# A two-layer GELU network on one core: the engines' instructions emitted without a block

## The chip, the core and the metric

The kernel runs on one core of one Trainium2 chip. The metric is the device time of one execution in microseconds (us). A core has five engines with an instruction stream each: TensorE (PE), VectorE (DVE), ScalarE (ACT), GpSimd (POOL) and SyncE (SP). They meet only through semaphores; transfers between memory and the core's own buffers are DMAs that SP, ACT or POOL issue and that add to a semaphore when they land.

## What is computed

```python
def reference(x, w1, b1, w2, b2):          # x: 1 x 2048 x 448
    h = jnp.einsum("bsd,df->bsf", x, w1) + b1   # w1: 448 x 1792
    h = _gelu(h)                                # tanh approximation
    return jnp.einsum("bsf,fd->bsd", h, w2) + b2   # w2: 1792 x 448
```

All inputs and the output are bfloat16. There are 2048 tokens of 448 numbers, a hidden layer of 1792, and an output as large as the input.

## The kernel before

The first product makes the hidden layer transposed: 14 tiles of 128 hidden features by four chunks of 512 tokens, 56 tiles `g_sb` in all. TensorE accumulates each in one of eight PSUM banks (L265), ScalarE applies bias and GELU on the way to `g_sb` (L366). The depth of 448 is cut into three slices of 128 rows and one of 64, and the 64-row slices of two tiles are paired, so that each pair of tiles costs seven passes. The second product takes 128 tokens at a time: 14 matmuls over the hidden features (L339), then VectorE adds the second bias on the way to `out_sb` (L389), and a store goes out (`store`, L166 to L169). There are 16 token tiles; the last is cut into 320 and 128 columns, so that there are 17 stores. TensorE does the whole first product (`l1`), then the whole second (`l2` for the four chunks), in an order written out by hand.

The beginning is staged so that TensorE has work early. It runs twelve warm-up matmuls on constants (L238), then turns the first 512 tokens by matmuls with an identity matrix (L248), while the weights arrive; VectorE and ScalarE copy the turned tokens out of PSUM (L378, L362). POOL makes the identity (L224, L226) and issues one small DMA (L231). The other tokens come in through transposing DMAs.

SP issues nearly all transfers in this order: the first tokens (L207, L208), pieces of the first weights (L180, L185, L186, L189), the transposing loads (L199), the second weights (L193), the second bias (L216), and then, as each VectorE addition is done, the stores (L169) but for the last, which ScalarE issues (L371). SP's last act is the wait for all 17 stores (L220), 16 counts of `sem_od` each.

Constants and a first barrier of all engines are made when the program object is created (L406): POOL sets four constants; each engine drains and reports to a gathering semaphore; POOL waits for four reports and releases the four others.

Line 160 opens a block, and each engine's function is registered with it by a decorator (L205, L222, L233, L353, L373). The block is closed where the `with` of L121 ends. In the program as built, the main body then holds only the constants, the first barrier and one unconditional branch per engine; each engine's work is a body of its own that ends with another branch; and a common end body holds a second barrier of the same form as the first (a drain on each engine, POOL's two events, an event on each of the others). The instructions of that end carry line 121. SP's wait for the stores is attached to its branch to the end body.

Of the kernel before, what the change touches and what calls it, by code (L numbers as in the profile page):

```python
# [11 lines left out]
def bass_standalone__dense_activation_gelu__prompt_kernel(  # L12
# [78 lines left out]
    for i in range(OPENING, len(order), QUAD):  # L91
# [3 lines left out]
        steps += phase(i + 2, 0) + phase(i, 1) + phase(i + 2, 1)  # L95
    assert len(set(steps)) == len(steps)
    assert sum((1 + h // 2) * (t1 - t0) for _, h, _, (t0, t1) in steps) == len(order) // 2 * 7 * SC


# [5 lines left out]
    for n, (i, h, m, _) in enumerate(steps):  # L105
        before = ahead.get(i)
        turn.append(before if before is not None and {steps[before][1], h} == {0, 1} else None)
        ahead[i] = n
        starts.append(before is None)
# [11 lines left out]
    with ExitStack() as es:  # L121
# [35 lines left out]
        sem_osb = S_("sem_osb")  # L157
        sem_od = S_("sem_od")

        block = es.enter_context(nc.Block())  # L160


        x0_view = x2[0:SC, :].rearrange("(p t) d -> p t d", t=STC)
        out0_view = out2[0:SC, :].rearrange("(p t) d -> p t d", t=STC)
# [1 line left out]
        def store(eng, n):  # L166
            j, c0, c1 = outs[n]
            to = out0_view[:, j, c0:c1] if j < STC else out2[j * P:(j + 1) * P, c0:c1]
            eng.dma_start(to, out_sb[:, j, c0:c1]).then_inc(sem_od, 16)  # L169

        def x_part(n, parts):
            h, k = parts[0]
            to = xT_sb[:, k:k + len(parts), 2 * h * P:2 * (h + 1) * P]
            src = ps[XBANK[n]][:, 0:2 * P * len(parts)]
            return to, src.rearrange("p (k t) -> p k t", k=len(parts))

        def load_w10(eng, i):
            a, b = W0_PIECES[i]
            with nc.allow_non_contiguous_dma(reason="w1 column pieces"):
                eng.dma_start(w1_sb[:, 0, a * P:b * P], w1[0:P, a * P:b * P]).then_inc(sem_w10[i], 16)  # L180

        def load_w1(eng):
            with nc.allow_non_contiguous_dma(reason="w1 column pieces"):
                for k, r in list(enumerate(KROW))[1:]:
                    eng.dma_start(w1_sb[:, k, 0:WCUT], w1[r:r + P, 0:WCUT]).then_inc(sem_w1[k], 16)  # L185
                eng.dma_start(  # L186
                    w1_sb[:, 0:3, WCUT:F], w1[0:3 * P, WCUT:F].rearrange("(k p) f -> p k f", p=P)
                ).then_inc(sem_w1r, 16)
                eng.dma_start(w1_sb[:, 3, WCUT:F], w1[KROW[3]:D, WCUT:F]).then_inc(sem_w1r, 16)  # L189

        def load_w2(eng, i):
            a, b = W2_PIECES[i]
            eng.dma_start(  # L193
                w2_sb[:, a:b, :], w2[a * P:b * P, :].rearrange("(ft p) d -> p ft d", p=P)
            ).then_inc(sem_w2[i], 16)

        def load_xT(eng, c):
            for k, d0 in enumerate(KROW):
                eng.dma_start(  # L199
                    xT_sb[:, k, c * SC:(c + 1) * SC],  # L200
                    x2[c * SC:(c + 1) * SC, d0:d0 + P],
                    transpose=True,
                ).then_inc(sem_x[c], 16)

        @block.sync  # L205
        def _(sp):
            sp.dma_start(xn_sb[:, 0:2, :], x0_view[:, 0:2, :]).then_inc(sem_xn[0], 16)  # L207
            sp.dma_start(xn_sb[:, 2:4, :], x0_view[:, 2:4, :]).then_inc(sem_xn[1], 16)  # L208
            load_w10(sp, 1)
            load_w1(sp)  # L210
            load_xT(sp, 1)
            for c in range(2, NSC):
                load_xT(sp, c)
            for i in range(len(W2_PIECES)):
                load_w2(sp, i)
            sp.dma_start(b2_bc[:, :], b2.partition_broadcast(P)).then_inc(sem_b2, 16)  # L216
            for n in range(len(outs) - 1):
                sp.wait_ge(sem_osb, n + 1)
                store(sp, n)
            sp.wait_ge(sem_od, 16 * len(outs))  # L220

        @block.gpsimd  # L222
        def _(pool):
            pool.memset(ident[:, :], 0.0).then_inc(sem_id, 1)  # L224
            pool.wait_ge(sem_id, 1)
            pool.affine_select(  # L226
                out=ident[:, :], in_=ident[:, :], compare_op=ALU.not_equal, fill=1.0,
                base=0, pattern=[[-1, P]], channel_multiplier=1,
            ).then_inc(sem_id, 1)

            pool.dma_start(b1n_sb[NFT:SQ, :], w1[0:SQ - NFT, 0:P]).then_inc(sem_b1x, 16)  # L231

        @block.tensor  # L233
        def _(pe):
            ones_w = nc.const_aps.tensor(1.0, [P, P], BF16)
            ones_x = nc.const_aps.tensor(1.0, [P, WN], BF16)
            for _i in range(NWARM):
# [90 lines left out]
            def l2(c):  # L328
                pe.wait_ge(sem_g, NFT * (c + 1))
                for n, (j, c0, c1) in enumerate(outs):  # L330
                    if j // STC != c:
                        continue
                    free("o", n)
                    for ft in range(NFT):
                        if j == 0:
                            for i, (a, _) in enumerate(W2_PIECES):
                                if ft == a:
                                    pe.wait_ge(sem_w2[i], 16)
                        mm = pe.matmul(  # L339
                            bank("o", n)[:, 0:c1 - c0],  # L340
                            lhsT=g_sb[:, ft, j * P:(j + 1) * P],
                            rhs=w2_sb[:, ft, c0:c1],
                            start=(ft == 0), stop=(ft == NFT - 1),
                        )
                    mm.then_inc(sem_l2, 1)
# [4 lines left out]
            for c in range(NSC):  # L350
                l2(c)

        @block.scalar  # L353
        def _(act):
            act.dma_start(b1n_sb[0:NFT, :], b1.rearrange("(c p) -> c p", p=P)).then_inc(sem_b1n, 16)
            load_w10(act, 0)
            zero = nc.const_aps.tensor(0.0, [P, 8], FP32)
            act.activation(act_junk[:, :], zero, ACT.Gelu_apprx_tanh)  # L358
            for n, (e, parts) in enumerate(XPARTS):
                if e == "a":  # L360
                    act.wait_ge(sem_xtp, n + 1)
                    act.copy(*x_part(n, parts)).then_inc(sem_xTa, 1)  # L362
            act.wait_ge(sem_b1, 1)
            for i, (c, ft) in enumerate(order):
                act.wait_ge(sem_l1, i + 1)
                act.activation(  # L366
                    g_sb[:, ft, c * SC:(c + 1) * SC], bank("g", i)[:, :], ACT.Gelu_apprx_tanh,
                    bias=b1_f[:, ft:ft + 1], scale=1.0,
                ).then_inc(sem_g, 1)
            act.wait_ge(sem_osb, len(outs))  # L370
            store(act, len(outs) - 1)  # L371

        @block.vector  # L373
        def _(dve):
            for n, (e, parts) in enumerate(XPARTS):
                if e == "d":
                    dve.wait_ge(sem_xtp, n + 1)
                    dve.tensor_copy(*x_part(n, parts)).then_inc(sem_xTd, 1)  # L378
            dve.wait_ge(sem_b1n, 16)
            dve.wait_ge(sem_b1x, 16)  # L380
            for q in range(P // SQ):
                to = slice(q * SQ, (q + 1) * SQ)
                dve.transpose(b1t_sb[to, :], b1n_sb[:, to]).then_inc(sem_b1T, 1)  # L383
            dve.wait_ge(sem_b1T, P // SQ)
            dve.tensor_copy(b1_f[:, :], b1t_sb[:, 0:NFT]).then_inc(sem_b1, 1)  # L385
            dve.wait_ge(sem_b2, 16)
            for n, (j, c0, c1) in enumerate(outs):
                dve.wait_ge(sem_l2, n + 1)
                dve.tensor_tensor(  # L389
                    out=out_sb[:, j, c0:c1], in0=bank("o", n)[:, 0:c1 - c0], in1=b2_bc[:, c0:c1],  # L390
                    op=ALU.add,
                ).then_inc(sem_osb, 1)


# [26 lines left out]
```

## Time and profile before

| | us |
|---|---|
| median of three runs | 94.45 (94.42 to 94.81) |
| the profiled execution | 93.88 |
| its span, first to last instruction of the program | 92.1 |
| TensorE busy | 89.1 |
| ScalarE busy | 36.6 |
| VectorE busy | 12.2 |

The span is shorter than the execution's time because the runtime has work of its own around the program. TensorE's granted clock was 1.00 throughout. In the profile's rows, a group is named by source line, engine, operation and tiles (out<-in), then a count; PEld is TensorE's loading of weights, which overlaps its matmuls; a name with a q behind it (SPq, ACTq) is an engine's sequencer, which waits, branches and issues DMAs and is not counted as busy. The chain of waits is followed back from the last instruction: each piece is shown with its start, its length and what ran. In the view of one line's instructions, the three numbers are the shortest, median and longest duration in ns, followed by the first and last start in us. Times are counted from the first instruction of the program. Apart from instructions, the trace holds the time of every update of a semaphore, those of the runtime ahead of the program and behind it too.

### The profile page before, as it was taken

Reading aid. Unit: us, or ns where it says so; the run is one execution under the profiler, and the core shown is the slowest. Engines: PE = TensorE matmul, PEld = TensorE weight load, DVE = VectorE, ACT = ScalarE, POOL = GpSimd, SP = SyncE. Lnnn points to the kernel's source line nnn. Section 1 sums busy time; section 2 is a strip of 40 time slices with the busy share of each in tenths; the row PEclk is TensorE's granted clock in tenths of the full one; section 3 lists DMA queues with packets and bytes.
Section 4 is the critical chain, followed back from the end, with each engine's and each line's share of the span. In section 5 each row is a group of like instructions: output and inputs, shape, how many; then the busy total and the mean of one; then the engine's idle time right before and its main releaser. Section 6 shows DMA issues by size and latency. Waiting matters only on the chain.

```text
span 92.1 us, 1498 instructions
## 1 busy us (share of the span) xinstructions
PE 89.1 (97%) x650; PEld 47.2 (51%) x650; DVE 12.2 (13%) x25; ACT 36.6 (40%) x61; POOL 1.4 (1%) x7
## 2 busy tenths in 40 slices
PE   6999999999999999999999999999999999999990
PEld 4664445555555555555545555555555555555570
DVE  0260000000000000000001112222211222222131
ACT  2640999877887779777973000000000000000000
POOL 5000000000000000000000000000000000000000
PEclk9999999999999999999999999999999999999999
DMA  1999988554893000000000111101111110011111
GB/s 24 343 332 333 154 148 73 114 108 74 271 368 104 0 0 4 7 0 0 0 0 0 50 57 50 42 7 50 50 50 50 50 50 29 28 50 50 50 50 50
DMA packets 12562, 7.52 MB, mean 82 GB/s; under 512 B 7171, under 2 KB 12172, under 8 KB 12556
## 3 DMA queue, kind: packets, MB, share of 16 engines
q1 hardware_dynamic: 12208, 7.26, 31.1%
q10 hardware_dynamic: 316, 0.17, 0.6%
q8 instruction: 5, 0.08, 0.3%
q0 software_dynamic: 32, 0.00, 0.1%
q14 instruction: 1, 0.01, 0.0%
HBM read 4.02 MB, written 1.84 MB: 64 GB/s over the span
## 4 chain that ended last, share of the span: by engine, by line
PE 97%; DVE 0%; issue 0%
PE ps L265 46%; PE ps L339 46%; PE ps L238 3%; PE ps L248 1%; DVE out_sb L389 0%
## 5 line engine op out<-in xcount | busy, mean ns | idle before, releaser
L265 PE MATMUL ps<-xT_sb,wi_sb 64*128 64x512 bf16 (+2 forms) x384 | 42.8, 374 | 0.0
L339 PE MATMUL ps<-wo_sb,g_sb 128*128 128x448 bf16 (+2 forms) x238 | 42.6, 341 | 0.0
L366 ACT ACTIVATE g_sb<-ps,bi_f 128x512 bf16<-128x512 f32 x56 | 33.7, 694 | 9.5 <-PE ps L265 9.5
L339 PEld LDWEIGHTS ps<-wo_sb,g_sb 128*128 128x128 bf16 x238 | 22.7, 98 | 20.1 <-issue 0.4
L265 PEld LDWEIGHTS ps<-xT_sb,wi_sb 64*128 64x128 bf16 (+1 forms) x384 | 21.7, 94 | 20.5 <-issue 0.6
L389 DVE TENSOR_TENSOR out_sb<-ps,bo_bc 128x448 bf16<-128x448 f32 (+2 forms) x17 | 10.1, 597 | 73.8 <-PE ps L339 73.8
L238 PE MATMUL ps<-const-bfloat16-1.0 128*128 128x256 bf16 x12 | 2.7, 413 | 0.8 <-PEq L406 0.8
L238 PEld LDWEIGHTS ps<-const-bfloat16-1.0 128*128 128x128 bf16 x12 | 1.6, 140 | 1.4 <-issue 0.8
L358 ACT ACT_TABLE_LOAD x1 | 1.3, 1283 | 1.8 <-issue 1.8
L362 ACT CAST xT_sb<-ps 128x512 bf16<-128x512 f32 (+1 forms) x3 | 1.4, 516 | 1.2 <-PE ps L248 1.2
L378 DVE CAST xT_sb<-ps 128x256 bf16<-128x256 f32 x3 | 1.2, 421 | 4.1 <-PE ps L248 3.9
L248 PEld LDWEIGHTS ps<-ident,xn_sb 128*128 128x128 bf16 x16 | 1.2, 112 | 0.5 <-issue 0.5
L248 PE MATMUL ps<-ident,xn_sb 128*128 128x128 bf16 x16 | 1.4, 244 | 0.0
L383 DVE STREAM_TRANSPOSE bit_sb<-bin_sb 32x32 bf16<-32x32 bf16 x4 | 0.8, 200 | 0.1
L231 POOL DMA_DIRECT2D bin_sb<-in_w_dram x1 | 0.7, 657 | 0.2 <-issue 0.2
L226 POOL TENSOR_SCALAR_AFFINE_SELECT ident<-ident 128x128 bf16<-128x128 bf16 x1 | 0.3, 287 | 0.2 <-POOL ident L224 0.2
L358 ACT ACTIVATE act_junk<-const-float32-0.0 128x8 bf16<-128x8 f32 x1 | 0.2, 209 | 0.0
L224 POOL MEMSET ident<- 128x128 bf16 x1 | 0.2, 204 | 0.3 <-POOLq L406 0.3
L385 DVE CAST bi_f<-bit_sb 128x14 f32<-128x14 bf16 x1 | 0.2, 176 | 0.0
L406 POOL MEMSET const-float32-0.0<- 128x1 f32 x1 | 0.1, 99 | 0.2 <-issue 0.2
L406 POOL MEMSET const-bfloat16-1.0<- 128x1 bf16 x1 | 0.1, 102 | 0.0
L406 POOL MEMSET const-uint8-127<- 128x1 uint8 x1 | 0.1, 102 | 0.0
(1 smaller groups left out, 0.1 us busy)
## 6 DMA issues: line engine op xcount, KB each, us to landing
out_dram<-out_sb SPq DMA_DIRECT2D x15, 112.0 KB, 1.7
wo_sb<-in_w_dram SPq DMA_DIRECT2D x2, 784.0 KB, 6.0
wi_sb<-in_w_dram SPq DMA_DIRECT2D x3, 256.0 KB, 4.0
wi_sb<-in_w_dram SPq DMA_DIRECT2D x1, 576.0 KB, 6.4
xn_sb<-in_x_dram SPq DMA_DIRECT2D x2, 224.0 KB, 2.7
wi_sb<-in_w_dram SPq DMA_DIRECT2D x1, 192.0 KB, 6.6
xT_sb<-in_x_dram SPq DMA_TRANSPOSE x12, 3.6
wi_sb<-in_w_dram ACTq DMA_DIRECT2D x1, 128.0 KB, 2.9
```

Of the source, the lines that this page charges most:

```text
L231: pool.dma_start(b1n_sb[NFT:SQ, :], w1[0:SQ - NFT, 0:P]).then_inc(sem_b1x, 16)
L238: pe.matmul(ps[0][:, 0:WN], lhsT=ones_w, rhs=ones_x, start=True, stop=True)
L248: mm = pe.matmul(ps[XBANK[n]][:, col:col + P], lhsT=xn_sb[:, 2 * h + t, KROW[k]:KROW[k] + P], rhs=ident[:, :], start=True, stop=True,)
L265: return pe.matmul(bank("g", i)[:, t0:t1], lhsT=w1_sb[lo:hi, k, ft * P:(ft + 1) * P], rhs=xT_sb[lo:hi, k, c * SC + t0:c * SC + t1], start= ...
L339: mm = pe.matmul(bank("o", n)[:, 0:c1 - c0], lhsT=g_sb[:, ft, j * P:(j + 1) * P], rhs=w2_sb[:, ft, c0:c1], start=(ft == 0), stop=(ft == NF ...
L358: act.activation(act_junk[:, :], zero, ACT.Gelu_apprx_tanh)
L362: act.copy(*x_part(n, parts)).then_inc(sem_xTa, 1)
L366: act.activation(g_sb[:, ft, c * SC:(c + 1) * SC], bank("g", i)[:, :], ACT.Gelu_apprx_tanh, bias=b1_f[:, ft:ft + 1], scale=1.0,).then_inc( ...
L378: dve.tensor_copy(*x_part(n, parts)).then_inc(sem_xTd, 1)
L383: dve.transpose(b1t_sb[to, :], b1n_sb[:, to]).then_inc(sem_b1T, 1)
L389: dve.tensor_tensor(out=out_sb[:, j, c0:c1], in0=bank("o", n)[:, 0:c1 - c0], in1=b2_bc[:, c0:c1], op=ALU.add,).then_inc(sem_osb, 1)
L406: nc = _bacc.Bacc("TRN2", target_bir_lowering=False, num_devices=1)
```

## The change

The block is not opened. The five decorated functions become plain functions that are called once each at the end of the kernel, with the engine as argument, so that their instructions stand in the program's main body. Within each engine, the order of the working instructions, their operands and their semaphores stay. In the program as built, the five branches into the engines' bodies, the five branches out of them and the end body's barrier (five drains, six events) are gone; the first barrier stays. SP's wait for the stores, which the branch to the end body carried, is an event instruction of its own, the last in SP's stream.

```diff
-        block = es.enter_context(nc.Block())
-
...
-        @block.sync
-        def _(sp):
+        def sync_work(sp):
...
             sp.wait_ge(sem_od, 16 * len(outs))
 
-        @block.gpsimd
-        def _(pool):
+        def gpsimd_work(pool):
...
-        @block.tensor
-        def _(pe):
+        def tensor_work(pe):
...
-        @block.scalar
-        def _(act):
+        def scalar_work(act):
...
-        @block.vector
-        def _(dve):
+        def vector_work(dve):
...
+        sync_work(nc.sync)
+        gpsimd_work(nc.gpsimd)
+        tensor_work(nc.tensor)
+        scalar_work(nc.scalar)
+        vector_work(nc.vector)
```

## The prediction

> **What bounds the kernel now.** I read the page first, then the chain of waits, then the last microseconds, because the change touches only how each engine enters and leaves its work. The page:
>
> ```profile
> span 92.1 us, 1498 instructions
> ...
> PE 89.1 (97%) x650; PEld 47.2 (51%) x650; DVE 12.2 (13%) x25; ACT 36.6 (40%) x61; POOL 1.4 (1%) x7
> ...
> q8 instruction: 5, 0.08, 0.3%
> q14 instruction: 1, 0.01, 0.0%
> ```
>
> TensorE is busy 97% of the span, so a change that leaves its matmuls alone can work only at the two ends. The chain that ended last, in order of time, ends so:
>
> ```profile
> 5.33 42.02 PE ps L265 x380
> 47.35 42.53 PE ps L339 x238
> 89.88 0.02 issue
> 89.90 0.29 DVE out_sb L389
> ```
>
> The chain has no hole between 0.79 and 90.19. What is left is 0.79 us ahead of it and 92.10 - 90.19 = 1.91 us behind it. The timeline of the end and the instructions of line 121, which is where the block is closed (POOLq, SPq and so on are the sequencers):
>
> ```profile
> 89.90 0.29 DVE L389 TENSOR_TENSOR out_sb<-ps,bo_bc 128x128 bf16<-128x128 f32 x1 [0.29 <-PE ps L339]
> 90.22 0.35 ACTq L169 DMA_DIRECT2D out_dram<-out_sb  x1
> ```
>
> ```profile
> L121 POOLq EVENT_SEMAPHORE  x2: 17/17/17, 91.9 to 92.0; - x2
> ...
> L121 SPq COMPARE_BRANCH  x1: 33/33/33, 91.7 to 91.7; - x1
> L121 SPq DRAIN  x1: 7/7/7, 91.9 to 91.9; - x1
> L121 SPq EVENT_SEMAPHORE  x1: 17/17/17, 92.0 to 92.0; - x1
> L121 ACTq EVENT_SEMAPHORE  x1: 17/17/17, 92.0 to 92.0; - x1
> ...
> L121 PEldq EVENT_SEMAPHORE  x1: 51/51/51, 92.0 to 92.0; - x1
> ```
>
> And what SP waited for:
>
> ```profile
> SPq L121 <- DMA out_dram<-out_sb: 1.7, 1, 1.7
> ...
> SPq L121 <- PEq L121: 0.2, 1, 0.2
> ```
>
> The reader is to see a ladder. The last store is issued at 90.22 and lands at 91.71 (semaphore updates in the trace); SP's branch, which carries the wait for the stores, runs at 91.727; SP's drain at 91.883; POOL, which gathers the five engines, at 91.916 and 91.994; the four others are let go at 92.036 to 92.047; TensorE's event ends the span at 92.098. Everything from 91.727 on is the block's end and does no work.
>
> **The start.** The change removes one branch per engine behind the first barrier. That barrier (line 406) stays. I cost the branch at nothing, because it isn't there: the trace has no branch record on any engine at the start, and PE's first weight load starts 77 ns after the barrier's event (0.679 to 0.756), exactly what lies between event and weight load at 3.421, 4.403, 7.656 and 11.669 inside PE's stream, where there is no branch. The other engines show 85 ns (SP) and 88 ns (ACT) from event to first DMA issue, and 119 ns on POOL from the release to the first memset. The nearest rows without a branch are ACT's 68 ns from an event to an activation and POOL's 79 ns between its two events. So the bounds of the gain are 0 and 0.04 us, and even that is behind cover: PE's twelve warm-up matmuls (line 238) start the chain and run until 3.5 us whatever POOL, SP and ACT do. Below nothing there is no reason in the rows. I take 0.
>
> The Trainium skill, "Runtime: NRT & Kernel Launch", section "Instruction fetch mechanics", says that a taken branch to code outside the current window forces a fetch before the engine can go on, so by it five removed branches could each be worth a fetch. The 77 ns above is against it here.
>
> **The end within the span.** What goes: SP's branch as a carrier of the wait (a plain event takes its place, 17 ns by SP's row), SP's drain, POOL's two events, the events of the other four, and drains and branches of engines that are done earlier anyway (DVE's drain starts at 89.916, ACT's at 90.618, under the cover of the store's landing). New end: 91.727 + 0.017 = 91.744. Removed from the span: 92.098 - 91.744 = **0.354 us**. The stall that remains is the store's flight, 90.22 to 91.71, which the change leaves alone.
>
> **The end behind the span.** The profiled execution took 93.88 us, 1.78 us more than its span. The trace shows what follows: semaphore 2, which no line of the kernel uses, gets nine updates from 92.337 to 92.871; all semaphores are cleared in five batches between 92.77 and 93.43; semaphore 2 gets nine more from 93.656 to 94.014. The same nine updates stand ahead of the program, from -0.371 to 0.001. I read each nine as a barrier that goes through the five engines in a row and back. The steps ahead of the program took 0.372 us, the second nine 0.358 us, but the first nine behind it 0.534 us: there, the third update comes 0.215 us after the second, against 0.038 in both others. One engine was late by 0.177 us. The program's barrier lets all five go within 0.03 us, so they all run their way out at the same time and the slowest is felt. After the change four of them have left long before (PE at 89.9, DVE 90.2, ACT 90.6, POOL in the first microseconds), and only SP's way out is on the path.
>
> How much that adds depends on SP's place in the row, which no record names. PE's way out, from its event's end to the first update, is 92.337 - 92.098 = 0.239 us; I take it for SP.
> - SP first in the row: 91.744 + 0.239 + 0.372 = 92.355 against 92.871, a gain of 0.52.
> - SP fifth, at the turn: the others wait there already, and what is left after the fifth update is 92.871 - 92.653 = 0.218: 91.744 + 0.239 + 0.218 = 92.201, a gain of 0.67.
> - SP is itself the late third: its way out is 92.586 - 92.053 = 0.533, then 92.871 - 92.586 = 0.285: 92.562, a gain of 0.31.
>
> The batches of clears favour the fifth: the first batch, of semaphores 207 to 255, starts at 92.77, before the row is through, the one of 3 to 53 last, at 93.08; PE is also the engine that enters the program last (0.316, against 0.000 for SP). So PE stands at the ends of the row and SP at the turn. I take **0.65 us**, near that end. The rest (clears, second barrier) I take as unchanged.
>
> The skill's same page, section "The ~15µs preamble/postamble breakdown", gives about 1.5 us for the barrier behind a kernel and 44 ns a hop. The hops agree with 0.372 / 8 = 0.047 us; of the 1.5 us, this trace shows 0.77 (92.098 to 92.871). If that stage had a fixed length, only the 0.354 us of the span would be gained.
>
> **The sum.** 93.88 - 0.65 = 93.23 us for an execution like the profiled one. That one is 0.57 us under the median of the runs shown; the gain carries over, so 94.45 - 0.65 = **93.80 us**, 0.7% less. A difference of 0.5% (0.47 us) is about what a measurement of this kernel can tell from no change; the gain is little more than that.
>
> **Rivals.**
> 1. Only the span shrinks: the first of the runtime's barriers takes as long as before behind SP (SP is the late engine, or the time measured doesn't reach into it). Then 94.45 - 0.35 = 94.10. For it: no record names the engines of the row, and the time measured is not a time of the trace. Against: 1.78 us lie outside the span, close to the 1.92 us from 92.098 to 94.014.
> 2. Nothing changes (94.45): the way out of SP has a cost which the block's barrier covered, such as a fetch of the code behind the program that now starts only when SP gets there. SP's step from branch to drain, 0.156 us, and POOL's way out, 92.586 - 92.011 = 0.575, bound such a cost; at 0.575 for SP in place of 0.239, the gain of 0.67 falls to 0.33, and one such step more takes it to nothing.
> 3. Slower: instruction refills come into the open. The page's five packets of q8 hold 16 KB each and take 0.3% x 16 x 92.1 / 5 = 0.9 us each; I take them for TensorE's stream, the one engine with enough instructions (its 650 loads and 650 matmuls would have some 60 bytes each). With three to five instructions fewer per engine the boundaries move against the work. One refill wholly exposed gives 94.45 - 0.65 + 0.9 = 94.70; two give 95.6. It decides from the point where PE stands idle for more than 0.65 us in all. Against: PE has no hole near any of the five (13.4, 28.0, 38.4, 53.5, 77.5), the stream is as straight as before, and a shift of four instructions, two loads with their matmuls, is 2 x 42.53 / 238 = 0.36 us of its pace.
>
> **How the numbers follow.** My forecast, 93.80, has 0.56 (own range 93.55 to 94.0); rival 1, 0.22; rival 2, 0.13; rival 3, 0.09. Faster by over 0.5% means below 93.98: nearly all of the first case and a small part of rival 1 whose run-to-run spread reaches there, 0.55. Slower by over 0.5% means above 94.92: the part of rival 3 with more than one refill, and spread as of the 94.81 among the runs shown, 0.06. The rest, 0.39, is within. The range, 93.5 to 94.6, takes in the forecast's low side (SP's way out nearly free, a gain of 0.67 + 0.24 = 0.91, so 93.54) and reaches over rivals 1 and 2 up to 94.6; beyond is most of rival 3.
>
> **What would show it.** In the changed kernel's profile the block's line is gone; the first weight load of PE still starts 77 ns after the barrier's event; the chain to the last DVE addition has the same length within 0.3 us; the last record is SP's event some 20 ns after the last landing, and the span is near 91.75. In the semaphore records the nine updates behind the span have no gap of 0.2 us at the third, and the ninth comes about 0.45 us after the span's end, against 0.77 now. A hole in PE's row, a later last addition, or a longer stretch from SP's event to the clears would make me wrong.

## The result and the profile after

The changed kernel takes 93.70 us (median of 18 runs, 93.12 to 94.23) against 94.44 us before (18 runs, 94.09 to 94.89). The ratio is 0.992, with a 95% interval of 0.990 to 0.994: faster by 0.8%. By this ratio it is 0.77 us, with an interval of 0.55 to 0.97 us; the medians are 0.74 us apart. 93.80 had been forecast.

The page of the changed kernel's profiled execution (94.23 us):

```profile
span 92.9 us, 1487 instructions
...
PE 89.3 (96%) x650; PEld 47.5 (51%) x650; DVE 12.2 (13%) x25; ACT 36.7 (40%) x61; POOL 1.4 (1%) x7
```

The kernel became faster, and its span is 0.8 us longer than in the profile of before. That is a trap: an execution is not the median. The chain of waits of that execution shows why (start, length, what):

```profile
...
2.13 5.03 DMA wi_sb<-in_w_dram
7.16 0.05 issue
7.20 41.33 PE ps L260 x374
48.53 42.53 PE ps L334 x238
91.06 0.02 issue
91.08 0.29 DVE out_sb L382
```

The timeline has the wait itself (in brackets, the idle time and what ended it):

```profile
5.18 1.03 PE L260 MATMUL ps<-xT_sb,wi_sb 128*128 128x256 bf16 x6
...
7.20 1.04 PE L260 MATMUL ps<-xT_sb,wi_sb 128*128 128x512 bf16 x4 [0.99 <-DMA wi_sb<-in_w_dram]
```

TensorE stood from 6.21 to 7.20, waiting for a piece of the first weights that landed at 7.16; in the profile of before, that piece was there at 5.96. The experiments show that this isn't the change's doing. Behind the opening, the work is the same: the second product again takes 42.53 us.

The two ends are what the change touches. The start is the same. In the trace's records, in us: PE's first weight load at 0.755 (before 0.756), SP's first issue at 0.752 (0.752), ACT's at 0.749 (0.759), POOL's memset at 0.745 (0.745). At the end, one instruction is left where twelve records of line 121 stood, and SP waits for the stores as long as it did, 1.7 us from the end of its own last issue, with no wait behind it. (The last store, which ScalarE issues, lands 1.49 us after its issue, before and after.)

```profile
L217 SPq EVENT_SEMAPHORE  x1: 17/17/17, 92.9 to 92.9; - x1
```

```profile
SPq L167 <- DVE out_sb L382: 62.2, 16, 28.7
SPq L217 <- DMA out_dram<-out_sb: 1.7, 1, 1.7
...
```

Counted from the landing of the last store, with the nine updates of semaphore 2 which I had read as the runtime's first barrier behind the program:

| us from the last landing | before | after |
|---|---|---|
| span's end | 0.387 | 0.033 |
| updates 1 to 4 | 0.626, 0.660, 0.875, 0.919 | -1.640, -0.857, -0.819, -0.775 |
| update 5 | 0.942 | 0.155 |
| updates 6 to 9 | 1.039, 1.077, 1.113, 1.160 | 0.198, 0.236, 0.270, 0.318 |
| last of the second nine | 2.303 | 1.466 |

Four updates came well before the stores landed; only the fifth waits for SP. The ninth comes 0.842 us earlier. Of this, 0.354 us lie in the span, 0.488 behind it. From the ninth update to the last it is 1.14 us and 1.15 us.

The time less its span says the same of many runs, not of two: its median is 1.80 us in 33 runs of the kernel before (taken with the experiments), 1.31 us in the 18 runs of the changed one and 1.33 in its second set. So the measured time reaches over the runtime's first barrier behind the program, and 0.47 to 0.49 us of the gain lie there.

### The profile page after: what moved, and what is told of

Read it like the earlier page. It is cut to its first block, busy times and chain, and to the rows that moved or that the text cites. A ratio compares the mean times of both kernels' runs of the same rounds, so it can differ in the third digit from the quotient of the medians.

```text
span 92.9 us, 1487 instructions
## 1 busy us (share of the span) xinstructions
PE 89.3 (96%) x650; PEld 47.5 (51%) x650; DVE 12.2 (13%) x25; ACT 36.7 (40%) x61; POOL 1.4 (1%) x7
## 4 chain that ended last, share of the span: by engine, by line
PE 90%; DMA 5%; SPq 1%; DVE 0%; issue 0%
PE ps L334 46%; PE ps L260 44%; DMA wi_sb<-in_w_dram 5%; SPq L178 0%; SPq L205 0%; SPq L204 0%; DVE out_sb L382 0%
## 5 line engine op out<-in xcount | busy, mean ns | idle before, releaser
L243 PE MATMUL ps<-ident,xn_sb 128*128 128x128 bf16 x16 | 1.6, 257 | 0.0
L243 PEld LDWEIGHTS ps<-ident,xn_sb 128*128 128x128 bf16 x16 | 1.3, 117 | 0.4 <-issue 0.4
```

The costliest lines, as they stand in the source:

```text
L243: mm = pe.matmul(ps[XBANK[n]][:, col:col + P], lhsT=xn_sb[:, 2 * h + t, KROW[k]:KROW[k] + P], rhs=ident[:, :], start=True, stop=True,)
```

## The experiments

An engine's way out is, from here on, the time from the end of its last instruction to its update of semaphore 2. My theory was that the gain is all behind the last landing: the block's end barrier is paid twice, once in the span, and once more because it sends all five engines into the runtime's barrier at nearly the same moment, where the slowest way out and the whole row are felt. The rivals: the branches and the straight stream are the gain; SP's own shorter end is; GpSimd's drain is; the load stage moved.

**The changed kernel again** (no edit).

> The changed kernel once more, for its ends on this chip. Theory (the gain is all behind the last store's landing: 0.355 us of span and 0.488 us in the runtime's first barrier): from the last landing to the ninth update of semaphore 2 there are 0.32 us, as in the first profile (92.89 to 93.21), and 1.15 us more to the last of all; the ratio to the kernel before is 0.991 (0.84 / 94.4). Rival (the load stage moved with the change): PE waits over 1 us for a piece of the first weights again, as at 6.2 to 7.2 in the first profile. Theory: that wait differs from one execution to another and is mostly shorter.

Measured: ratio 0.991 (0.987 to 0.996). Ninth update 0.329 us from the landing, the last of all 1.176 us after that. In this execution, the chain has no wait for the weights:

```profile
...
4.85 0.89 PE ps L260 x4
5.74 0.22 PE ps L243 x4
5.96 42.08 PE ps L260 x380
48.04 42.53 PE ps L334 x238
...
```

The 0.99 us of the first profile are gone from the chain with nothing changed. The work behind them starts only half of that earlier (the 64th matmul at 10.27 in place of 10.77), since other steps of the opening took longer: the sixteen matmuls of L243 took 285 ns on average, against 257. The tail stays to 0.04 us; the opening doesn't stay.

**A barrier put back, without block and branches.**

```diff
         vector_work(nc.vector)
+        nc.all_engine_barrier()
```

> The changed kernel with a barrier of all engines as its last instructions, in the main body, no block and no branch. Theory (the barrier is the price, the branches are nothing): the tail comes back, 0.31 us from the landing to the span's end in place of 0.03, and 0.77 us from there to the ninth update of semaphore 2 in place of 0.29; 93.7 + 0.77 = 94.5, a ratio to the kernel before of 1.000. Rival (branches and the straight stream are the gain): stays at 93.7, 0.992.

Measured in the trace: 0.293 us from the landing to the span's end, 0.774 from there to the ninth update, as expected; time less span 1.79 us, as before the change. The gap in the runtime's barrier is back too: third update 0.185 us after the second. But the median was 94.83 us, ratio 1.004 (1.000 to 1.008), 0.3 more than expected, and the median span 93.05 against 92.7 of the kernel before. What was too long lay in the opening. Hence the next run.

The barrier's rows show the ladder of line 121 again, under the line that calls it (the drains that end earlier are left out):

```profile
L393 POOLq EVENT_SEMAPHORE  x2: 17/17/17, 92.9 to 93.0; - x2
...
L393 SPq DRAIN  x1: 7/7/7, 92.9 to 92.9; - x1
L393 SPq EVENT_SEMAPHORE  x1: 17/17/17, 93.0 to 93.0; - x1
...
L393 PEldq EVENT_SEMAPHORE  x1: 51/51/51, 93.0 to 93.0; - x1
```

Its first rung is shorter: SP goes from the start of its event to its drain in 0.060 us, where its branch took 0.156. So of the 1.160 us from the landing to the ninth update, the branch that carried the wait cost 0.093 (1.160 - 1.067), and the barrier 0.749 (1.067 - 0.318).

**The same kernel again.**

> The same kernel as end_barrier, once more. There its tail cost what was expected, but its median was 0.32 us over the kernel before, where the tail is 0.09 us shorter; the rest of that (0.4 us) lay in the opening, up to the 64th matmul, after which all traces agree within 0.02 us. Theory (the opening's length is the luck of a load of the program): the median comes to 94.4, ratio 0.999, the tail as before (0.29 us in the span, 0.77 behind it). Rival (a barrier in the main body makes the opening longer): again 94.8, 1.004.

Measured: 94.52 us, ratio 0.999 (0.996 to 1.002); tail 0.299 and 0.772 us. The surplus of the first time didn't come again. With the barrier put back, the gain is gone, and the branches left out brought no more than the interval allows. The rival of the straight stream falls, but for the 0.09 us of the branch that carried the wait, which the times are too coarse to show.

**POOL leaves with SP.**

```diff
         vector_work(nc.vector)
+        nc.gpsimd.wait_ge(sem_od, 16 * len(outs))
```

> The changed kernel with POOL waiting for the stores too, as its last instruction; SP waits as before, no barrier. Theory (GpSimd is the late engine of the runtime's barrier, its way out 0.575 us): the span is the same, the third of the nine updates comes 0.58 us behind the span's end and the ninth 0.285 after it, 0.86 in place of 0.29; 93.7 + 0.57 = 94.27, ratio 0.998. Rival (the gain behind the span comes from SP's shorter end, no drain and no branch, not from the others' early leaving): no change, 93.7, 0.992.

Measured: 94.08 us, ratio 0.996 (0.993 to 1.000). That is 0.19 us under the 94.27 expected, and 0.15 of it lies in the opening: the median span less its tail is 92.16, against 92.31 in the kernel before. The span's end stays at 0.041 us from the landing, with one more event in it, which runs 8 ns after SP's:

```profile
L393 POOLq EVENT_SEMAPHORE  x1: 17/17/17, 92.0 to 92.0; - x1
```

The updates from the landing: -1.673, -0.862, then 0.586, 0.630, 0.653, 0.750, 0.790, 0.824, 0.871. The third is the late one, 0.545 us behind the span's end, and the ninth comes 0.285 after it: 0.83 in all, 0.86 expected. One wait of 17 ns, which delays no work and moves the span by 0.008 us, takes back 0.55 us behind it; time less span is 1.87 us. So GpSimd stands third, and its leaving late is by itself enough to lose all that the change gains behind the span. The reverse doesn't follow: the next run shows that TensorE's leaving late costs too, and no run lets GpSimd alone leave early. The rival of SP's shorter end falls for what lies behind the span: SP's end is here as short as in the changed kernel.

**TensorE leaves with SP; ScalarE leaves with SP.** The same line with `nc.tensor` and with `nc.scalar`.

> The changed kernel with TensorE waiting for the stores too, as its last instruction; SP waits as before, no barrier. Theory (TensorE stands first in the row of the runtime's barrier, its way out 0.239 us): the first of the nine updates comes 0.24 us behind the span's end and the ninth 0.37 after it, 0.61 in place of 0.29, and the span is 0.03 longer for TensorE's event of 51 ns; 93.7 + 0.36 = 94.06, ratio 0.996. Rival (only GpSimd is slow on its way out and the places in the row do not matter): within 0.05 us of 93.7.

> The changed kernel with ScalarE waiting for the stores too, as its last instruction. Theory (places in the row decide; ScalarE is second): the first update is early, the second comes 0.2 to 0.27 us behind the span's end and the ninth 0.335 after the second, so 0.53 to 0.6 from the span's end in place of 0.29; ratio 0.994 to 0.995. Rival (ScalarE is not in the row's second place): the ninth comes with another distance from the first late update: 0.25 if it is fourth.

Measured: TensorE 94.13 us, ratio 0.995 (0.992 to 0.999); ScalarE 93.85 us, 0.995 (0.992 to 0.998). The updates from the landing:

| leaves last, beside SP | first late update | from the span's end | ninth, from the span's end | time less span |
|---|---|---|---|---|
| nobody | fifth, 0.155 | 0.122 | 0.285 | 1.31 |
| ScalarE | second, 0.147 | 0.108 | 0.431 | 1.48 |
| TensorE | first, 0.271 | 0.190 | 0.549 | 1.59 |
| GpSimd | third, 0.586 | 0.545 | 0.830 | 1.87 |
| all (kernel before) | first, 0.626 | 0.239 | 0.773 | 1.80 |

The places are as read: TensorE first, ScalarE second, GpSimd third, SP at the turn. VectorE's fourth place is what is left over; no run lets it leave last. The prices don't add up, they cover each other: with GpSimd late 0.545 us more than with nobody late, with TensorE 0.264, with ScalarE 0.146, with all at once 0.488 (there GpSimd is let go 0.087 us before the span's end). The sizes were a little smaller than expected: TensorE's way out is 0.190 us here, not 0.239 (so 0.55 for the ninth, expected 0.61), ScalarE's 0.108 (0.43, expected 0.53 to 0.60; a miss, since I had taken its way out from a bound). The last two columns move together: in each row the time less the span is the ninth update and 1.02 to 1.05 us. This ties the trace's updates to the measured time, better than the medians of the whole time do, in which the opening's spread stands too.

**The block without GpSimd's drain.**

```diff
-        block = es.enter_context(nc.Block())
+        block = es.enter_context(nc.Block(no_gpsimd_drain=True))
```

> The kernel before with the block's end barrier without GpSimd's drain; branches, the other drains and the events stay. Theory (what costs is that all engines leave together): the tail is that of before, 0.39 us from the landing to the span's end and 0.77 us to the ninth update; 94.5, ratio 1.000. Rival (GpSimd is late in the runtime's barrier because of its drain): the third of the nine updates comes without the gap, 0.18 us are gained, ratio 0.998.

Measured: 94.86 us, ratio 1.003 (1.000 to 1.007). The gap stands, third update 0.219 us after the second, and the ninth 0.771 us behind the span's end. The drain isn't what makes GpSimd late. The span's end moved out to 0.468 us from the landing, 0.08 more than expected, as this barrier has an instruction more between SP's drain and the gathering. The rest of the 0.36 us over the 94.5 expected lies in the opening: the median span less its tail is 92.6, against 92.3 in the kernel before.

```profile
L121 SPq EVENT_SEMAPHORE  x2: 17/17/17, 92.7 to 92.9; - x2
...
L121 SPq COMPARE_BRANCH  x1: 33/33/33, 92.5 to 92.5; - x1
L121 SPq DRAIN  x1: 7/7/7, 92.7 to 92.7; - x1
```

**The kernel before again** (no edit, one execution).

> The kernel before once more, for the length of its opening and its tail. Theory: from the 64th matmul to the last 80.05 us as in all traces, 1.16 us from the landing to the ninth update, 1.14 us more to the last; the opening (64th matmul at 9.60 in the first profile) differs by up to 1 us. Rival (the first profile's opening is that of the block): again 9.6.

Measured: landing to ninth update 1.170 us, then 1.148 to the last. The start of the 64th matmul (counted from nought) and the stretch from there to the last one:

| | 64th matmul at | to the last matmul |
|---|---|---|
| before, twice | 9.60, 9.69 | 80.05, 80.19 |
| after, twice | 10.77, 10.27 | 80.05, 80.07 |
| barrier put back, twice | 10.68, 10.75 | 80.05, 80.05 |
| POOL, TensorE, ScalarE late | 9.87, 10.18, 9.85 | 80.05, 80.05, 80.05 |
| block without the drain | 10.36 | 80.05 |

From the 64th matmul on, the kernels can't be told apart (the 80.19 is the one execution with a granted clock of 0.999). All that differs ahead of the tail lies in the first 11 us, by up to 1.2 us. The two profiles of before both had short openings, which by itself speaks for the rival. The spans of many runs decide here, not the ten profiles: the median span less the tail in it is 92.7 - 0.39 = 92.3 us before (33 runs) and 92.35 - 0.03 = 92.3 after (18 runs; 92.4 in the second set). The change leaves the opening as it was. Its length goes with one landing: the piece of the first weights that TensorE waited for in the first profile (the first of L183's three, L185 before) landed at 5.91 to 7.16 us, and the 64th matmul started 3.62 to 3.96 us behind it in nine of the ten profiles, 4.27 in that with TensorE late. Why this landing varies stays open.

## Why the prediction was right

- **The start at nothing**: right. Four first instructions start within 0.010 us of where they did. With the barrier put back, the kernel without branches at the start is as slow as before. The Trainium skill's rule that a taken branch to code outside the current window forces a fetch ("Runtime: NRT & Kernel Launch", "Instruction fetch mechanics") finds no case in these runs. The 75 to 77 ns from event to first weight load with the branch (three profiles) were 76 to 77 ns without it (seven). This comparison is what holds; the four rows of 77 ns in the prediction were picked from a stream in which others lie between 7 and 186 ns.
- **The span's 0.354 us**: right to the last digit, in two profiles (end 0.033 and 0.034 us behind the landing). The experiments split it: 0.09 to 0.10 is the branch as carrier of the wait, the rest the barrier's ladder.
- **0.30 us behind the span, to make 0.65**: the mechanism was right, the size too small. 0.488 was measured in the trace, 0.842 in all, and the interval of the times, 0.55 to 0.97 us, holds both 0.65 and 0.842. The ninth update came 0.285 us after the span's end, where about 0.45 was forecast. The tail's 0.842 us alone would have made 93.60 of 94.44; the 93.70 measured lies between that and the forecast, so that the nearness of 0.10 us is no measure of how well the tail was sized.
- **The two terms that were mis-sized**: SP's way out, taken from TensorE as 0.239 us, is 0.122. And 0.218 us from the turn to the end is 0.163, because the step from the fifth update to the sixth shrinks from 0.097 to 0.043 us. It is 0.097 or 0.098 in the eight profiles where the fourth update came only 0.023 or 0.024 us before the fifth, and 0.043 or 0.044 in the two where it came 0.93 or 0.94 us before. I read this so: an engine that already waits passes the update on sooner than one that has just given its own. 0.117 + 0.055 = 0.172, which added to the 0.67 worked out for the fifth place gives 0.84. One reading was off without weight in the sum: the program's barrier lets the five engines go within 0.05 us (91.994 to 92.047), not 0.03.
- **SP at the turn**, chosen from the order of the clears: right. In the changed kernel, four updates are early and the fifth is the first late one; first (0.52) and third (0.31) are taken by TensorE and GpSimd. The reason held as well: in all ten profiles the first batch of clears starts 0.113 to 0.129 us behind the fifth update.
- **Rival 1**, only the span shrinks: excluded by the time less the span, 1.80 to 1.31 us. The Trainium skill's 1.5 us for the barrier behind a kernel ("Runtime: NRT & Kernel Launch", "The ~15µs preamble/postamble breakdown") is no fixed price here: the stretch from the span's end to the ninth update took 0.29 to 0.83 us, by who left last. **Rival 2**, a cost that the block had covered: none shows; SP's way out was shorter, not longer. **Rival 3**, refills in the open: the trace's five refills lie at 15.6 to 78.5, and from the 64th matmul on nothing moved by more than 0.02 us.
- **What would show it**: the span near 91.75 and the chain's same length came in neither profile (92.9 and 92.4 us, the last addition 1.18 and 0.69 us later), because the profile of before had a short opening. I had named a hole in PE's row as a sign against me; it was one of the opening's, and a second profile and 51 spans were needed to say so.

## What to carry to other kernels

In this kernel a barrier at the end of the program was paid twice, as the runtime has one of its own behind it: once for its own ladder (some 0.26 of the 0.354 us), and again because it held back engines that could have gone through the runtime's row under the flight of the last store (0.488 us). So let each engine end when its work ends, and let a single engine wait for the stores, one whose way out is short and that stands far back in the row: here SP. Where the change is at the ends, compare the ends, counted from a common event such as the last landing; the span of one execution can move the other way.

## What was not expected of the hardware

- The engines' ways out of a program differ: 0.11 us (ScalarE), 0.12 and 0.13 (SP), 0.19 (TensorE), 0.545 (GpSimd), from the end of the last event to the update of the runtime's semaphore. SP's are from two executions of the changed kernel, the others from one each with that engine late. Behind a barrier, in five profiles, TensorE took 0.235 to 0.269 and GpSimd 0.575 to 0.576. One wait on GpSimd that ends with the stores costs 0.55 us, though it holds up nothing in the kernel.
- A branch that carries a wait took 0.156 to 0.160 us to the next instruction on SP, an event 0.060. A branch at the start, from one body to the next in the same stream, left no record and cost nothing that can be seen.
- The opening's length varied by 1.2 us between executions and by 0.3 us in the median time of two sets of twelve runs of one kernel (94.83 and 94.52), against 0.77 us that the change brings.
